# Three taps of one convolution on GpSimd, and the first superblock's weights widened in two halves

## The chip, the cores and the metric

The kernel runs on one core of a Trainium2 chip. The time is that of the whole device program in microseconds, the median of three runs. The engines are named as the profile names them: PE (TensorE matmul), PEld (its weight loads), DVE (VectorE), ACT (ScalarE), POOL (GpSimd), SP (SyncE, which issues the transfers).

## The reference

A causal convolution of seven taps over a sequence, with softmax weights by head (8 heads of 24 channels), is followed by an MLP with a squared ReLU:

```
w = softmax(weight)                    # (8 heads, 7 taps)
out = einsum('hk,bskhg->bshg', w, x_unf)   # x: (8, 4096, 192), padded by 6 in front
h = out.reshape(32768, 192) @ w_in     # 192 x 2048
g = s * relu(h)**2 + b
y = g @ w_out                          # 2048 x 192
```

All of it is float32; the weights of the MLP reach the kernel as the 64-bit words of float64 numbers.

## The kernel before, in words

Each operand of a matmul is split into a high and a low part (`hi`, `lo`, in the type fp32r), and three products (hi by hi, lo by hi, hi by lo) stand for one in float32. The 32768 tokens are worked on in 32 superblocks of 1024 tokens, each of two blocks of 512 columns. The 2048 hidden features are eight pairs of 256. For a block `j` and a pair `p`, `first(n, j, p)` makes the hidden values of 256 features with 18 half-height matmuls into one of two buffers `h`; ACT takes ReLU (`relu`) and the square (`square`); ACT or DVE casts to `qh`; DVE subtracts to get `ql` (`lows`); and `second` (in superblock 0 `second_whole`, ten matmuls) multiplies by `w_out` and accumulates over the pairs. A queue holds the second products back by two items (`LAG`).

Superblock 0 is different from the other 31. Its 90 us hold, beside its own products, the widening of all weights: class `Widen` takes the 64-bit words of one pair (768 columns of words: 384 of `w_in`, 384 of `w_out`) and makes hi and lo. Its steps are `magnitudes` (ACT: absolute value of the upper words into a tile `t`), a clamp to the float32 range (DVE, line 308), two bit operations (DVE, lines 312 and 315; these three are `top`), `his` (ACT: `t` cast into the high half of `W` and `WB`), `low` (DVE, lines 328 and 329) and `los` (DVE, lines 335 and 337, once for `W` and once for `WB`). `W` holds `w_in` and the first 128 output columns of `w_out`, `WB` the last 64. `first(0, j, p)` needs the `w_in` part of pair `p`, `second_whole(0, j, p)` the `w_out` part, `WB` first.

`head` is the start: tap weights by softmax, the convolution of the B channels (64 channels of both blocks, `accB`) on PE as seven float32 products with diagonal matrices, that of block 0's A channels (`acc0`) on DVE as seven operations, and that of block 1's A channels (`acc1`) on PE again, seven products. `split_A` and `split_tensor` make hi and lo of them; `swap` exchanges the two halves of the partitions by transfers (`wA`, `wB`). `pair(p)` then does pairs 2 to 7. `CONV` says how many steps of superblock 1's convolution (17 in all, on DVE) are done in which pair, and `TWICE` names the pairs that have no second products of their own behind them, so that two pairs of `first` follow each other on PE.

DVE, ACT and PE run what is written for superblock 0 in just the order in which it is written (`in_order`); POOL's instructions are placed by the scheduler. An engine executes its own list in order, so an instruction that waits holds all behind it. `raw` holds two tiles `t` and one `c`; `wordp` three tiles of words; `ps_h` two buffers `h`.

Of the kernel before, what the change touches and what calls it, by code (L numbers as in the profile page):

```python
# [9 lines left out]
F32 = mybir.dt.float32  # L10
# [7 lines left out]
P = 128  # L18
# [5 lines left out]
CONV = (0, 1, 1, 1, 1, 1, 4, 8)  # L24
# [13 lines left out]
def conv_attention_then_squared_relu_mlp(  # L38
# [244 lines left out]

    class Widen:
# [15 lines left out]
        def magnitudes(self):  # L300
            self.t = raw.tile([P, CT], I32, name="t")[:, self.lo : self.hi]

            top = words[self.p][:, self.lo : self.hi, 1]
            nc.scalar.activation(self.t.bitcast(F32), top.bitcast(F32), AF.Abs)

        def top(self):
            t, top = self.t, words[self.p][:, self.lo : self.hi, 1]
            nc.vector.tensor_scalar(
                t.bitcast(F32), t.bitcast(F32), TOP_MIN, TOP_MAX, op0=ALU.max, op1=ALU.min
            )  # L310

# [12 lines left out]
        def low(self):  # L324
            low = words[self.p][:, self.lo : self.hi, 0]
            c = raw.tile([P, CT], I32, name="c", bufs=1)[:, self.lo : self.hi]
# [6 lines left out]
        def los(self):  # L333
            for hi, lo, t in self.parts(self.t.bitcast(F32)):
                nc.vector.tensor_tensor(lo, t, hi.bitcast(F32), op=ALU.subtract)
            for _, lo, f in self.parts(self.f):
                nc.vector.tensor_tensor(lo, lo.bitcast(F32), f, op=ALU.add)

        def rest(self):
            self.low()  # L340
            self.los()
# [4 lines left out]
    def fetch(p, a=0, z=None):  # L346
# [19 lines left out]
    nc.vector.reduce_max(tmax, tap, axis=AX.X)  # L366
    nc.vector.tensor_tensor(
        tap, tap, tmax.unsqueeze(2).to_broadcast([P, 2, K]), op=ALU.subtract
    )
    nc.scalar.activation(tap, tap, AF.Exp)  # L370
    nc.vector.reduce_sum(tsum, tap, axis=AX.X)
# [9 lines left out]
    def head():  # L381
# [9 lines left out]
        w0, w0out, w1 = Widen(0, 0, CI), Widen(0, CI, CT), wide[1]  # L391

        def diagonal(w):
            d = act.tile([P, 2, BLK], F32, name="q").rearrange("p a (k f) -> p (a k) f", f=P)
            for k in range(K):
                nc.scalar.activation(d[:, k, :], ident, AF.Identity, scale=w[:, k : k + 1])
            return d

        top, bottom = slice(0, DB), slice(DB, P)
        diagB = diagonal(tapB)  # L400
# [3 lines left out]
        acc0 = xs.tile([P, BLK], F32, name="accA")  # L404
        for _ in one.conv(acc0, one.xA, tapA, BLK):
            pass
        nc.scalar.mul(minus, ident, -1.0)
        diagA = diagonal(tapA)
        w0.magnitudes()
        split = one.split_A(0, acc0)  # L410
        next(split)
        w0.top()
        w0.his()
# [3 lines left out]
        lo = one.split_tensor(accB, hiB, lambda: one.conv_tensor(acc1, diagA, one.xA[:, BLK:], range(0, 2)))  # L417
# [431 lines left out]
```

## Time and profile before

| | |
|---|---|
| time, median of three runs | 2234.87 us (2234.49 to 2235.01) |
| the profiled execution, first to last instruction | 2232.9 us |
| superblock 0, from the first instruction to the first product of superblock 1 | 90.2 us |
| one later superblock of 1024 tokens on PE (two blocks of 34.45 us) | 68.9 us |
| PE busy over the whole span | 2226.4 us |
| DVE, ACT, POOL busy over the whole span | 1753.5, 1286.4, 317.8 us |

The profile was taken on one execution, so its span may differ by some tenths of a microsecond from the runs' median; what lies around the span (start and end of the program) is about 2 us. A row of the timeline gives the start, the duration, the engine, the line of the kernel, the operation with output and inputs, and in brackets the idle time ahead of it with what ended it. Durations of instructions that follow each other on one engine overlap by some hundredths of a microsecond, so that the distance between two starts is what an instruction costs in a full list.

### The profile page before, as it was taken

The numbers are of one execution on the slowest core, as the hardware profiler recorded it, in microseconds if no ns is written. First come the engines' busy times: TensorE is split into PE (matmuls) and PEld (weight loads), VectorE is DVE, ScalarE is ACT, GpSimd is POOL, SyncE is SP. The second block draws the span as 40 slices with busy tenths as digits, with TensorE's granted clock in tenths as the row PEclk, the third lists the DMA queues.
The fourth block names the chain that finished last, engine by engine and source line by source line (L and its number), as shares of the span: only waits on it lengthen the run. The fifth ranks groups of instructions, "written<-read, shape, count | busy, mean of one in ns | idle before, by whom it ended". The sixth has DMA issues, their size and how long they took to land.

```text
span 2232.9 us, 45081 instructions
## 1 busy us (share of the span) xinstructions
PE 2226.4 (100%) x19330; PEld 1829.1 (82%) x19330; DVE 1753.5 (79%) x1995; ACT 1286.4 (58%) x1410; POOL 317.8 (14%) x205
## 2 busy tenths in 40 slices
PE   9999999999999999999999999999999999999999
PEld 6788888888888888888888888888888888888887
DVE  8898778777787787777877878778777787787764
ACT  8755555655555555555555555555655555556554
POOL 0022101111011011110110111111101111011110
PEclk9999999999999999999999999999999999999999
DMA  5113112121121111211111111112121121111110
GB/s 180 34 43 87 40 46 62 48 58 44 44 58 53 53 44 45 56 53 53 43 51 50 53 53 53 48 43 62 51 55 44 44 58 53 53 44 42 46 39 17
DMA packets 46168, 117.51 MB, mean 53 GB/s; under 512 B 7760, under 2 KB 8016, under 8 KB 45968
## 3 DMA queue, kind: packets, MB, share of 16 engines
q1 hardware_dynamic: 45824, 114.50, 18.6%
q8 instruction: 151, 2.47, 0.5%
q14 instruction: 49, 0.40, 0.1%
q10 hardware_dynamic: 144, 0.13, 0.0%
HBM read 31.64 MB, written 25.17 MB: 25 GB/s over the span
## 4 chain that ended last, share of the span: by engine, by line
PE 98%; DVE 1%; ACT 1%; DMA 0%; issue 0%; SPq 0%; DVEq 0%
PE acc L614 50%; PE h L531 46%; DVE accA L163 0%; PE acc L576 0%; ACT q L552 0%; DVE ql L559 0%; PE acc L577 0%; PE acc L583 0%; PE acc L582 0%; PE acc L581 0%; ACT qh L554 0%; ACT q L545 0%; DMA xA<-in_xA 0%; DVE t L315 0%; ACT oC L589 0%
## 5 line engine op out<-in xcount | busy, mean ns | idle before, releaser
L545 ACT ACTIVATE q<-h 128x1024 f32<-128x1024 f32 x512 | 525.5, 1026 | 902.8 <-PE h L531 900.4
L559 DVE TENSOR_TENSOR ql<-q,qh 128x1024 fp32r<-128x1024 f32 x512 | 656.7, 1283 | 56.3 <-ACT qh L554 2.6
L554 DVE CAST qh<-q 128x1024 fp32r<-128x1024 f32 x497 | 370.1, 745 | 395.7 <-ACT q L552 393.3
L614 PE MATMUL acc<-qh,W 64*128 64x512 f32 x3960 | 609.9, 386 | 0.0
L552 ACT ACTIVATE q<-q 128x1024 f32<-128x1024 f32 x512 | 543.6, 1062 | 15.9
L614 PEld LDWEIGHTS acc<-qh,W 64*128 64x128 f32 x3960 | 370.9, 184 | 77.9
L531 PE MATMUL h<-sA,W 64*128 64x512 f32 x3072 | 432.4, 387 | 0.0
L531 PE MATMUL h<-wA,W 64*128 64x512 f32 x3072 | 431.6, 386 | 0.0
L531 PE MATMUL h<-tB,W 64*128 64x512 f32 x1536 | 429.9, 386 | 0.0
L531 PE MATMUL h<-wB,W 64*128 64x512 f32 x1536 | 429.9, 386 | 0.0
L614 PE MATMUL acc<-ql,WB 64*128 64x512 f32 x1980 | 385.7, 386 | 0.4 <-DVE ql L559 0.4
L614 PE MATMUL acc<-qh,WB 64*128 64x512 f32 x1980 | 385.6, 386 | 0.0
L614 PE MATMUL acc<-ql,W 64*128 64x512 f32 x1980 | 385.5, 386 | 0.0
L638 POOL TENSOR_TENSOR oB<-oB,oB 128x512 f32<-128x512 f32 x61 | 115.2, 1889 | 1672.7 <-ACT oB L637 1672.7
L163 DVE SCALAR_TENSOR_TENSOR accA<-xA,tap,accA 128x512 f32<-128x512 f32 x378 | 341.5, 903 | 6.8
L531 PEld LDWEIGHTS h<-sA,W 64*128 64x128 f32 x3072 | 287.3, 184 | 62.9 <-issue 1.1
L531 PEld LDWEIGHTS h<-wA,W 64*128 64x128 f32 x3072 | 287.8, 184 | 60.4
L531 PEld LDWEIGHTS h<-tB,W 64*128 64x128 f32 x1536 | 282.6, 184 | 40.5 <-issue 0.2
L531 PEld LDWEIGHTS h<-wB,W 64*128 64x128 f32 x1536 | 282.5, 184 | 20.1
L614 PEld LDWEIGHTS acc<-ql,WB 64*128 64x128 f32 x1980 | 185.5, 184 | 40.1 <-DVE ql L559 1.3
L614 PEld LDWEIGHTS acc<-ql,W 64*128 64x128 f32 x1980 | 185.5, 184 | 39.0
L614 PEld LDWEIGHTS acc<-qh,WB 64*128 64x128 f32 x1980 | 185.5, 184 | 38.8
(115 smaller groups left out, 1035.4 us busy)
## 6 DMA issues: line engine op xcount, KB each, us to landing
wA<-sA SPq DMA_DIRECT2D x126, 256.0 KB, 3.6
outT<-oA SPq DMA_DIRECT2D x63, 256.0 KB, 2.0
wB<-tB SPq DMA_DIRECT2D x60, 256.0 KB, 3.4
xA<-in_xA SPq DMA_DIRECT2D x24, 515.0 KB, 3.6
xB<-in_xB SPq DMA_DIRECT2D x32, 259.0 KB, 2.6
oC<-oB SPq DMA_DIRECT2D x61, 128.0 KB, 2.2
outT<-oC SPq DMA_DIRECT2D x60, 128.0 KB, 2.3
words<-in_w SPq DMA_DIRECT2D x7, 768.0 KB, 6.2
```

The lines of the kernel that those rows point to most:

```text
L163: nc.vector.scalar_tensor_tensor(acc, src, w[:, k : k + 1], acc, op0=ALU.mult, op1=ALU.add)
L531: nc.tensor.matmul(h[:, i, :], w_in(w, p, chunk[0], rows), chunk[part], start=start, stop=stop)
L545: nc.scalar.activation(q, h, AF.Relu)
L552: nc.scalar.activation(q, q, AF.Square)
L554: cast(qh, q)
L559: nc.vector.tensor_tensor(ql, q, qh.bitcast(F32), op=ALU.subtract)
L614: nc.tensor.matmul(accs[to + 2 * i], w(f, r), q[r, f % 2, :], start=start and f == 0, stop=stop and f == ends[i],)
L638: nc.gpsimd.tensor_tensor(o[1], o[1], o[3], op=ALU.add)
```

## The change

In `head`, three of the seven taps of block 1's A channels (taps 4 to 6) are multiplied and summed by POOL into a tile `rest`; PE does four products with diagonal matrices and a fifth with the identity that adds `rest`. The order around it is new: the low part of block 0, the first high halves and the first of the four products are written in another order, and the high and low halves of pair 1's `w_in` come within `second_block`. The softmax takes the maximum as a bias and the sum from the activation's accumulator.

`Widen` is split: each pair is widened as `w_in` (384 columns) and `w_out` (384 columns) apart, with `top`, `his`, `low` and `los` for each. The clamp becomes a method of its own, `bound`, and is done by POOL for all but the first two `w_in` halves. The last addition of a `w_out` half's `los` (two instructions) is done by POOL too. In `pair(p)` the `w_in` half of the next pair is widened ahead of the `w_out` half of pair `p` itself; before, whole pairs were widened ahead. `CONV` gives pairs 1 and 2 none and the last two one more each.

```diff
-CONV = (0, 1, 1, 1, 1, 1, 4, 8)
+CONV = (0, 0, 0, 1, 1, 1, 5, 9)
+ON_PE = 4
...
+        def bound(self, engine=None):
+            t = raws[self.p][:, self.lo : self.hi].bitcast(F32)
+            (engine or nc.vector).tensor_scalar(
+                t, t, TOP_MIN, TOP_MAX, op0=ALU.max, op1=ALU.min
+            )
...
-        def los(self):
+        def los(self, engine=None):
             for hi, lo, t in self.parts(self.t.bitcast(F32)):
                 nc.vector.tensor_tensor(lo, t, hi.bitcast(F32), op=ALU.subtract)
             for _, lo, f in self.parts(self.f):
-                nc.vector.tensor_tensor(lo, lo.bitcast(F32), f, op=ALU.add)
+                (engine or nc.vector).tensor_tensor(lo, lo.bitcast(F32), f, op=ALU.add)
...
+        for k in range(ON_PE, K):
+            src = x1[:, k : k + BLK]
+            if k == ON_PE:
+                nc.gpsimd.tensor_scalar(rest, src, tapA[:, k : k + 1], None, op0=ALU.mult)
+            else:
+                part = outs.tile([P, BLK], F32, name="oA")
+                nc.gpsimd.tensor_scalar(part, src, tapA[:, k : k + 1], None, op0=ALU.mult)
+                nc.gpsimd.tensor_tensor(rest, rest, part, op=ALU.add)
...
-        one.conv_tensor(acc1, diagA, one.xA[:, BLK:], range(2, K))
+        lo = one.split_tensor(accB, hiB, lambda: on_tensor(range(0, 1)))
+        w0.his()
+        on_tensor(range(1, ON_PE))
+        nc.tensor.matmul(acc1, ident, rest, start=False, stop=True)
...
     def pair(p):
         ha, hb = first(0, 0, p), first(0, 1, p)
+        out = w_out_of[p]
+        out.bound(nc.gpsimd)
+        if p in TWICE:
+            qa, qb = relu(ha), relu(hb)
+            keep(p, 0, *square(qa, nc.scalar.copy))
+            out.top()
+            out.his()
+            out.low()
+            out.los(nc.gpsimd)
+            convolve(CONV[p] // 4)
+            keep(p, 1, *square(qb, nc.scalar.copy))
+            ready(p + 2)
+            convolve(CONV[p] - CONV[p] // 4)
+            return
+        last_pair = p == NPAIR - 1
+        if last_pair:
+            convolve(CONV[p] // 2)
+        else:
+            w_in_of[p + 1].top()
+            w_in_of[p + 1].low()
         qa = relu(ha)
+        if not last_pair:
+            w_in_of[p + 1].his()
+            w_in_of[p + 1].los()
+        two = p + 1 in TWICE
         qa = square(qa, nc.scalar.copy)
+        if not two:
+            keep(p, 0, *qa)
+        out.top()
+        qb = relu(hb)
+        out.low()
+        if two:
+            out.his()
+            out.los(nc.gpsimd)
+            ready(p + 2)
+            keep(p, 0, *qa)
+            qb = square(qb, nc.scalar.copy)
+            after = w_in_of[p + 2]
+            after.top()
+            after.low()
+            after.his()
+            after.los()
+        else:
+            nc.scalar.activation(qb, qb, AF.Square)
+            out.his()
+            out.los(nc.gpsimd)
...
+            ready(p + 2)
```

(`keep` appends an item with its `ql` to the queue; `ready(p)` is `magnitudes` of the whole pair `p` on ACT and `bound` of its `w_in` half on POOL.)

How this moves the instructions is seen at three places. The rows are those of the built programs; a number such as x2 counts equal neighbours, and line numbers differ between the two because the change adds lines.

On PE at the start of the program (`q` is a diagonal matrix, or the identity where the input is `accA`; `sA,W` are the first hidden products). Before:

```order
L257 MATMUL acc_139<-xB,q 128x512 x7
L257 MATMUL acc_140<-xA,q 128x512 x2
L230 MATMUL acc_139<-hiB,minus 128x512
L257 MATMUL acc_140<-xA,q 128x512 x5
L531 MATMUL h<-sA,W 128x512 x6
```

With the change:

```order
L259 MATMUL acc_139<-xB,q 128x512 x7
L438 MATMUL acc_140<-xA,q 128x512
L232 MATMUL acc_139<-hiB,minus 128x512
L438 MATMUL acc_140<-xA,q 128x512 x3
L445 MATMUL acc_140<-accA,q 128x512
L569 MATMUL h<-sA,W 128x512 x6
```

Seven products into `acc_140` have become five, and the last waits for POOL.

On ACT where pair 3 ends and pair 4 begins (`t<-words` are the magnitudes of pair 5, `W<-t` its high half, `q<-h` the ReLU of pair 4's two blocks, the other rows square and cast). Before:

```order
L304 ACTIVATE t<-words 128x768
L545 ACTIVATE q<-h 128x1024
L552 ACTIVATE q<-q 128x1024
L554 CAST qh<-q 128x1024
L322 CAST W<-t 128x640
L322 CAST WB<-t 128x2x64
L545 ACTIVATE q<-h 128x1024
L304 ACTIVATE t<-words 128x768
L545 ACTIVATE q<-h 128x1024
```

(the ReLU in the second row is still pair 3's, and the last magnitudes are those of pair 6). With the change:

```order
L309 ACTIVATE t<-words 128x768
L590 ACTIVATE q<-q 128x1024
L592 CAST qh<-q 128x1024
L332 CAST W<-t 128x384
L583 ACTIVATE q<-h 128x1024 x2
```

In both, pair 4's ReLUs stand behind the high half of pair 5. Before, three rows lay between its magnitudes and that high half, with DVE's three operations beside them; now two rows, with POOL's clamp and DVE's two bit operations beside them.

On DVE in pairs 6 and 7, the last of superblock 0 (`ql` is the low part of a hidden block, `accA` and `accB` are steps of superblock 1's convolution). Before:

```order
L559 TENSOR_TENSOR ql<-q,qh 128x1024
L163 SCALAR_TENSOR_TENSOR accA<-xA,tap,accA 128x512
L559 TENSOR_TENSOR ql<-q,qh 128x1024
L163 SCALAR_TENSOR_TENSOR accA<-xA,tap,accA 128x512
L180 TENSOR_TENSOR sA<-accA,sA 128x512
L161 TENSOR_SCALAR accB<-xB,tap 128x512
L163 SCALAR_TENSOR_TENSOR accB<-xB,tap,accB 128x512 x3
L559 TENSOR_TENSOR ql<-q,qh 128x1024
L163 SCALAR_TENSOR_TENSOR accB<-xB,tap,accB 128x512 x2
L559 TENSOR_TENSOR ql<-q,qh 128x1024
```

With the change, pair 6 and then, after the first steps into `accB`, pair 7:

```order
L597 TENSOR_TENSOR ql<-q,qh 128x1024
L322 TENSOR_SCALAR t<-t 128x384
L325 SCALAR_TENSOR_TENSOR t<-words,t 128x384
L338 TENSOR_SCALAR c<-t 128x384
L339 SCALAR_TENSOR_TENSOR c<-words,c 128x384
L345 TENSOR_TENSOR W<-t,W 128x256
L345 TENSOR_TENSOR WB<-t,WB 128x2x64
L165 SCALAR_TENSOR_TENSOR accA<-xA,tap,accA 128x512
L597 TENSOR_TENSOR ql<-q,qh 128x1024
L165 SCALAR_TENSOR_TENSOR accA<-xA,tap,accA 128x512 x3
L182 TENSOR_TENSOR sA<-accA,sA 128x512
```

```order
L597 TENSOR_TENSOR ql<-q,qh 128x1024
L322 TENSOR_SCALAR t<-t 128x384
L325 SCALAR_TENSOR_TENSOR t<-words,t 128x384
L338 TENSOR_SCALAR c<-t 128x384
L339 SCALAR_TENSOR_TENSOR c<-words,c 128x384
L345 TENSOR_TENSOR W<-t,W 128x256
L345 TENSOR_TENSOR WB<-t,WB 128x2x64
L165 SCALAR_TENSOR_TENSOR accB<-xB,tap,accB 128x512 x2
L597 TENSOR_TENSOR ql<-q,qh 128x1024
```

The `w_out` halves of pairs 6 and 7, six instructions each, now stand among the last low parts and the convolution; before, DVE had done them within pairs 4 and 5.

157 lines of the change are left out of this document (81 added, 76 removed).

## The prediction

> **What bounds the kernel now.** The page first: PE is busy in every slice. Then the windows by stage, which show where other engines are as full.
>
> ```profile
> PE 2226.4 (100%) x19330; PEld 1829.1 (82%) x19330; DVE 1753.5 (79%) x1995; ACT 1286.4 (58%) x1410; POOL 317.8 (14%) x205
> 17.30:31.70 14.40, 14.00 (x94) 10.54 (x93) 14.12 (x27) 13.59 (x19) 0.00 (x0) 1.00 0.82 280
> 67.90:90.10 22.20, 22.20 (x133) 17.83 (x132) 19.18 (x26) 16.41 (x19) 0.00 (x0) 1.00 0.13 35
> 165.00:2165.00 2000.00, 2000.00 (x17652) 1652.92 (x17650) 1572.91 (x1744) 1133.05 (x1223) 295.60 (x186) 1.00 0.19 51
> ```
>
> From 165 us on PE never idles, and the change touches nothing there. All it can move lies ahead of 90.2 us, in superblock 0, where DVE is 98% busy (14.12 of 14.40) at first and PE still idles 0.4. The chain of waits says how little room is there: it starts on DVE, not on PE, and leaves PE again at 72.34 for ACT and DVE until past 100 us.
>
> ```profile
> 5.06 0.50 DVE accA L161
> 14.06 0.48 DVE t L308
> 18.72 0.50 PE acc L230
> 67.97 4.35 PE h L531 x36
> 72.34 1.03 ACT q L545
> 79.40 0.62 ACT sA L178
> 86.27 1.22 DVE ql L559
> 90.12 0.69 ACT oA L587
> ```
>
> So PE is full, but without slack to DVE and ACT at the start (the low halves of the first weights) and in the tail of superblock 0. Those are the places the change rewrites.
>
> **The head, PE's side.** Five float32 products last from 12.96 to the start of the hidden products at 17.34, 0.88 us each; two fewer save 1.75. Between its first six products and the next, PE also waits for ACT's copy of `acc1` (18.72), about 0.8 us, which the new order can remove. At best 2.6.
>
> ```profile
> 12.96 4.46 PE L257 MATMUL acc<-xA,q 128*128 128x512 f32 x10
> 17.34 0.98 PE L531 MATMUL h<-sA,W 64*128 64x512 f32 x6
> 18.72 0.50 PE L230 MATMUL acc<-sA,minus 128*128 128x512 f32 x1 [0.40 <-ACT sA L227]
> 20.64 0.84 PE L531 MATMUL h<-sA,W 64*128 64x512 f32 x6
> ```
>
> **What POOL costs DVE.** POOL has not run beside DVE in superblock 0 so far. Later rows show both together:
>
> ```profile
> 1716.63 1.88 POOL L638 TENSOR_TENSOR oB<-oB,oB 128x512 f32<-128x512 f32 x1 [28.56 <-ACT oB L637]
> 1718.48 1.48 POOL L642 TENSOR_TENSOR oA<-oA,oA 128x512 f32<-128x512 f32 x1
> 1717.28 1.52 DVE L191 CAST hiB<-accB 128x512 fp32r<-128x512 f32 x1
> 135.07 0.41 DVE L191 CAST hiB<-accB 128x512 fp32r<-128x512 f32 x1
> 168.98 1.72 POOL L518 TENSOR_SCALAR oB<-oB,bias 64x512 f32<-64x512 f32 x1
> 162.00 3.07 DVE L163 SCALAR_TENSOR_TENSOR accA<-xA,tap,accA 128x512 f32<-128x512 f32 x3
> 81.18 2.33 DVE L163 SCALAR_TENSOR_TENSOR accB<-xB,tap,accB 128x512 f32<-128x512 f32 x3
> 167.49 1.78 DVE L180 TENSOR_TENSOR sA<-accA,sA 128x512 fp32r<-128x512 f32 x1
> ```
>
> An addition on POOL holds a DVE operation back by 1.1 us (1.52 against 0.41). A product with a scalar costs less: over four of them DVE loses 0.74 (3.07 against 2.33), 1.1 (1.78 for a subtraction of 0.69) and some tenths more on two others, about 0.6 each. By length I put a clamp of 384 columns at 0.45 of DVE's time and 1.25 of POOL's (1.67 between the starts at 512 columns; the lower end is 0.35, DVE's own), the two additions of 256 and 128 columns at 0.8 of DVE's and 1.1 of POOL's (from 1.48).
>
> [...]
>
> **The head, DVE's side.** DVE's list runs unbroken from 5.06, through block 0's convolution, to the low half of pair 0's `w_in` at 14.06. POOL can start when the second half of `xA` has landed:
>
> ```profile
> 1.65 3.28 DMA xA<-in_xA
> 2.60 0.43 SPq L153 DMA_DIRECT2D xA<-in_xA  x1
> xA<-in_xA SPq DMA_DIRECT2D x2, 256.0 KB, 3.8
> ```
>
> Two such transfers have a median of 3.8, and the first took 3.3, so the second took 4.3 from 2.60: 7.0 with the wake-up. Three products of 1.7 and two additions of 1.5 to 1.9 end near 16, so PE's fifth product ends near 17, not at 15.3: most of the 1.75 is spent there. DVE loses 3 x 0.6 + 2 x 1.1 = 4.0, and up to 2 x 0.45 for the clamps behind: low half at 18 to 19. Pair 1's `w_in` half follows:
>
> ```profile
> 10.19 0.35 DVE L308 TENSOR_SCALAR t<-t 128x384 f32<-128x384 f32 x1
> 10.97 0.56 DVE L315 SCALAR_TENSOR_TENSOR t<-words,t 128x384 int32<-128x384 int32 x1
> 12.05 0.35 DVE L328 TENSOR_SCALAR c<-t 128x384 int32<-128x384 int32 x1
> 13.50 0.56 DVE L337 TENSOR_TENSOR W<-W,c 128x384 fp32r<-128x384 f32 x1
> ```
>
> 1.3 (10.19 to the end at 11.5) and 2.0 (12.05 to 14.06) are 3.3: ready at 21.3 to 22.3. PE needs it at the fifth product of its second block, 0.45 behind 20.64 so far. That is +0.2 to +1.2; up to 1.0 more comes from ACT, whose cast of that half waits for DVE ahead of the copies that feed the second block's transfers. Ends: -2.6 (POOL blocks nothing) and +2.2. I take **+0.5**, since some blocks will fall on DVE's own waits.
>
> **Two pairs in a row on PE.** Behind pair 4, and again behind pair 6 (`TWICE`), the next pair's first product needs the buffer that ReLU frees, and ReLU stands behind the next pair's high half on ACT.
>
> ```profile
> 51.46 0.73 ACT L322 CAST W<-t 128x640 fp32r<-128x640 f32 x1 [0.40 <-DVE t L315]
> 52.37 1.03 ACT L545 ACTIVATE q<-h 128x1024 f32<-128x1024 f32 x1
> 54.21 1.03 PE L531 MATMUL h<-sA,W 64*128 64x512 f32 x6
> 54.74 0.18 PEld L531 LDWEIGHTS h<-sA,W 64*128 64x128 f32 x2 [0.34 <-DVE W L337]
> ```
>
> Before, that ReLU ended 0.8 ahead of PE's start at 54.21. Now DVE first widens the `w_out` half of pair 3, 0.8 + 0.9 + 0.5 = 2.2 us (by the rows above, 256 and 128 columns at 0.3 and 0.2); only then is a tile `t` free for pair 5's magnitudes. POOL does 1.1 of additions, then the clamp, 1.25; DVE 0.9; ACT's cast 0.45 and ReLU 1.05. That is 7.0 from the end of pair 4's `w_in` half. If that half is just in time for PE's pair 4, PE comes back after two blocks, 4.3 us (67.97 to 72.3), and waits 2.7; each microsecond that DVE is ahead takes one off. Ends 0 and 3.3; I take **+2.5** at each place, 5.0 together. This also bounds the gain: what PE saves in the head it gives back here, since DVE is not earlier by it.
>
> **The tail.** Pairs 6 and 7 get the `w_out` halves that DVE had done in pairs 4 and 5.
>
> ```profile
> 75.44 1.23 DVE L559 TENSOR_TENSOR ql<-q,qh 128x1024 fp32r<-128x1024 f32 x1 [1.06 <-ACT qh L554]
> 79.93 1.02 ACT L545 ACTIVATE q<-h 128x1024 f32<-128x1024 f32 x1
> 83.42 1.22 DVE L559 TENSOR_TENSOR ql<-q,qh 128x1024 fp32r<-128x1024 f32 x1
> 85.55 0.39 PE L576 MATMUL acc<-qh,WB 128*128 128x512 f32 x1
> 90.17 0.97 PE L531 MATMUL h<-sA,W 64*128 64x512 f32 x6
> ```
>
> Before: pair 7's first low part ends at 84.6, PE takes it at 85.55. Now, on the same chain: pair 6's `w_out` half puts its two bit operations (0.9) and ACT's cast (0.55) ahead of pair 6's second square, which with its low part comes 1.5 to 2.5 later; two more convolution steps stand ahead of `sA` (2 x 0.75), and ReLU of pair 7 behind it: low part 3.5 later. Behind it come pair 7's own `w_out` half, 2.2, and POOL's additions, 1.1, without which PE's product with `WB` cannot start. 3.5 + 3.3 - 0.95 of slack = 5.9, less what fell on idle time: **+5.5** (4.5 to 6.1). Last, ACT's final copy into `wB` now stands behind the output scaling that waits for the last product: **+0.8** (0 to 1.6) at the start of superblock 1. Nothing later gives it back: PE has no idle time there.
>
> **Sum.** 0.5 + 5.0 + 5.5 + 0.8 = 11.8 us, on a span of 2232.9: 2244.7. The runs' median is 2.0 above that span: **2246.7**. Moved for nothing: the softmax (DVE waits for `xA` until 5.06 anyway), the split of 768 into two 384 (some 0.5 a pair more) against the clamp and two additions less (1.1 a pair), which the blocks of 1.7 a pair outweigh.
>
> **The rivals.** *POOL is quick and blocks little.* Its clamps and additions are then near DVE's own times, the head keeps 2.6 and the place behind pair 4 costs nothing; behind pair 6 1.6 remains, and the tail with 4.5 to 5.5: +3.5 to +6, about 2239. For it: clamps with constants are not in the trace. Against: 1.72 for 512 columns. *DVE is blocked for POOL's whole record*: the head +4 to 5 more and the pairs a little, 16 to 21 in all, 2254. Against it, 1.52 against 0.41. [...] *PE stays the bound, on the other side*: the queue of two items hides the lateness of the tail, and two products and the wait are gone: -1.7 to -2.6, about 2232.6. It decides if pair 7's `w_out` half is ready within 1 us of its low part; DVE's list puts 2.2 and POOL 1.1 there. That the change does not do what it says is part of the first sum: POOL's `rest` comes after PE's four products.
>
> **How the numbers follow.** Forecast (+7 to +16) 0.57; POOL quick 0.18; whole-record block 0.10; PE stays the bound 0.15. What this kernel's measurement can tell from no change is about 0.2%, 4.5 us. Within it lie nearly all of the last and a third of the second: 0.19. Faster by more needs 4.5, more than the 2.6 there is: 0.02. Slower: 0.79. The range leaves out part of the gain below and half the whole-record case above: 2238 to 2254.
>
> **What would show it.** In the head: DVE's convolution of block 0 stretched beyond its 4.69, the fifth product near 16 and the first hidden product near 17, with PE waiting for a low half of `W`. Behind pairs 4 and 6: PE idle 2 to 3 us, released by ReLU. In the tail: PE idle 5 to 6 us at the first product with `WB` of pair 7, released by POOL. Wrong if PE's hidden products of superblock 1 start at or before 92, or if DVE keeps its durations beside POOL.

## The result and the profile after

The changed kernel takes 2257.5 us (median of four runs, 2256.5 to 2259.1) against 2234.8 (2234.5 to 2235.0): the ratio is 1.0102, with a 95% interval of 1.009 to 1.0114. It is slower by 22.7 us, where 11.8 had been forecast. The profiled execution is the run of 2259.1, 1.6 above the median; its span is 2257.4.

The loss lies where it was looked for, ahead of superblock 1: its first hidden product starts at 113.46 in place of 90.17. TensorE's waits up to 120 us, in the table of waits of the changed kernel (total, times, longest):

```profile
PE acc L614 <- POOL WB L347: 7.0, 2, 5.2
PE h L569 <- ACT q L583: 5.3, 2, 2.7
PE acc L445 <- POOL accA L421: 2.3, 1, 2.3
```

The same waits in the timeline of its PE (start, duration, operation, idle time ahead with what ended it):

```profile
17.33 1.18 PE L445 MATMUL acc<-accA,q 128*128 128x512 f32 x2 [2.31 <-POOL accA L421]
50.98 0.50 PE L614 MATMUL acc<-qh,WB 128*128 128x512 f32 x1 [1.85 <-POOL WB L347]
64.46 1.08 PE L569 MATMUL h<-sA,W 64*128 64x512 f32 x6 [2.67 <-ACT q L583]
86.83 1.65 PE L569 MATMUL h<-sA,W 64*128 64x512 f32 x6 [2.63 <-ACT q L583]
107.16 0.80 PE L614 MATMUL acc<-qh,WB 128*128 128x512 f32 x1 [5.19 <-POOL WB L347]
113.46 0.97 PE L569 MATMUL h<-sA,W 64*128 64x512 f32 x6
116.07 0.50 PE L569 MATMUL h<-wB,W 64*128 64x512 f32 x2 [0.95 <-ACT wB L216]
```

The gaps behind pairs 4 and 6 and the one in the tail have the forecast sizes. They are less than half of the loss. The ReLUs of superblock 0 on ACT show where the rest went. Before (pair 1's second block, pair 3's second block, the first block of pair 4 and of pair 7, superblock 1):

```profile
31.73 1.01 ACT L545 ACTIVATE q<-h 128x1024 f32<-128x1024 f32 x1
47.89 1.00 ACT L545 ACTIVATE q<-h 128x1024 f32<-128x1024 f32 x1
52.37 1.03 ACT L545 ACTIVATE q<-h 128x1024 f32<-128x1024 f32 x1
79.93 1.02 ACT L545 ACTIVATE q<-h 128x1024 f32<-128x1024 f32 x1
93.03 1.02 ACT L545 ACTIVATE q<-h 128x1024 f32<-128x1024 f32 x1
```

The same five in the changed kernel (pair 6's first ReLU, between, went from 70.30 to 85.76):

```profile
34.12 1.02 ACT L583 ACTIVATE q<-h 128x1024 f32<-128x1024 f32 x1
56.21 1.02 ACT L583 ACTIVATE q<-h 128x1024 f32<-128x1024 f32 x1
63.39 1.93 ACT L583 ACTIVATE q<-h 128x1024 f32<-128x1024 f32 x2
98.73 1.02 ACT L583 ACTIVATE q<-h 128x1024 f32<-128x1024 f32 x1
117.76 1.03 ACT L583 ACTIVATE q<-h 128x1024 f32<-128x1024 f32 x1 [1.74 <-PE h L569]
```

The lag grows from 2.4 (34.12 less 31.73) to 8.3 over pairs 2 and 3, where the forecast had nothing, to 11.0 at pair 4, 18.8 at pair 7 and 24.7 at superblock 1. What DVE does meanwhile is in the windows (DVE is the third busy time). Before, from 15 to 75 us and up to the first product of superblock 1:

```profile
15.00:75.00 60.00, 59.60 (x385) 45.09 (x385) 57.16 (x89) 54.16 (x68) 0.15 (x1) 1.00 0.35 122
0.00:90.17 90.17, 88.62 (x484) 63.51 (x484) 80.60 (x127) 75.78 (x106) 1.03 (x9) 1.00 0.36 120
```

Changed:

```profile
15.00:75.00 60.00, 53.08 (x300) 39.13 (x300) 45.52 (x76) 42.27 (x56) 29.27 (x24) 0.89 0.38 124
0.00:113.46 113.46, 97.46 (x480) 68.89 (x481) 87.17 (x143) 75.95 (x113) 46.02 (x44) 0.91 0.30 96
```

Two readings. DVE does not get less to do: it is busy for 87.2 us up to that product, 6.6 more than before, though clamps and additions have left it. And it idles 26.3 us (113.46 less 87.17) in place of 9.6: before, it was busy for 57.2 of the 60 us, nearly as full as PE (59.6); now for 45.5. The table of DVE's waits names the largest part:

```profile
DVE t L322 <- POOL t L315: 9.2, 6, 1.8
```

So DVE waits for POOL's clamp in six of the pairs. One more column had not been looked for: the granted clock (the number behind POOL's, 1.00 in every row of before). In the changed kernel it falls to half at five of the six gaps of PE (not at the one of 0.95 us):

```profile
19.00:25.00 6.00, 6.00 (x27) 4.00 (x25) 3.57 (x8) 3.59 (x7) 1.40 (x1) 0.50 0.70 154
52.00:56.00 4.00, 4.00 (x12) 3.12 (x11) 3.43 (x7) 2.22 (x3) 1.84 (x2) 0.57 0.01 5
66.00:70.00 4.00, 4.00 (x25) 3.13 (x24) 3.04 (x7) 1.81 (x4) 0.00 (x0) 0.57 0.00 0
86.50:90.00 3.50, 3.17 (x16) 2.52 (x18) 2.88 (x5) 3.18 (x4) 0.00 (x0) 0.51 0.00 0
107.00:111.00 4.00, 3.84 (x10) 3.08 (x11) 3.20 (x4) 0.00 (x0) 0.10 (x1) 0.57 0.02 4
```

The mean clock of 0.995 over the span of the profiled execution (0.996 and 0.997 in the other three) is 11 us' worth of full speed (0.005 x 2257), about what the forecast lacked. That made half speed the first suspect.

### The profile page after: what moved, and what is told of

It reads as the page before. It is cut to its first block, busy times and chain, and to the rows that moved or that the text cites. A ratio compares the mean times of both kernels' runs of the same rounds, so it can differ in the third digit from the quotient of the medians.

```text
span 2257.4 us, 45150 instructions
## 1 busy us (share of the span) xinstructions
PE 2235.8 (99%) x19326; PEld 1838.8 (81%) x19326; DVE 1760.6 (78%) x2012; ACT 1285.8 (57%) x1417; POOL 363.6 (16%) x240
## 4 chain that ended last, share of the span: by engine, by line
PE 95%; DVE 2%; POOL 1%; ACT 1%; DMA 0%; issue 0%; SPq 0%; DVEq 0%; POOLq 0%; ACTq 0%
PE acc L652 50%; PE h L569 45%; POOL t L315 0%; DVE ql L597 0%; DVE t L325 0%; POOL WB L347 0%; ACT q L590 0%; DVE t L322 0%; DMA xA<-in_xA 0%; ACT q L583 0%; POOL W L347 0%; ACT qh L592 0%; DVE c L339 0%; POOL oA L420 0%; DVE W L345 0%
## 5 line engine op out<-in xcount | busy, mean ns | idle before, releaser
L597 DVE TENSOR_TENSOR ql<-q,qh 128x1024 fp32r<-128x1024 f32 x512 | 660.7, 1291 | 57.2 <-ACT qh L592 3.7
```

What stands on the lines that cost most here:

```text
L597: nc.vector.tensor_tensor(ql, q, qh.bitcast(F32), op=ALU.subtract)
```

## The experiments

Times are medians, beside runs of the kernel before on the same chip (2234.6 to 2234.8 each time). Runs of one kernel lie within 2.7 us of each other, most within 1.

### Is it the clock?

Matmuls that multiply zeros into the accumulators fill PE's gaps (8 + 7 + 10 + 10 + 21; the sum in the expectation should read 56):

```diff
+        zeros_into(acc1, 8)
         nc.tensor.matmul(acc1, ident, rest, start=False, stop=True)
...
+        zeros_into(a2, ZEROS.get((j, p), 0))    # {(0, 1): 7, (0, 7): 21}
...
+        if p - 1 in TWICE:
+            zeros_into(acc[0, 0][0], 10)
```

> The changed kernel (2257.5 us), with 46 matmuls of 128 x 512 added that multiply zeros into the accumulators, put where its trace has TensorE idle while it waits: 8 before the fifth product of block 1 (the gap of 2.31 us), 7 before the wait of 1.85 us near 51 us, 10 before the first products of pairs 5 and 7 (2.67 and 2.63 us), 21 in the gap of 5.2 us near 102 us. At 0.227 us each they fill 1.8, 1.6, 2.3, 2.3 and 4.8 us and leave at most 0.5 us idle. Theory A (the time at half clock adds to the idle time): the granted clock stays at 1.00 in all five places, some 20 us at 0.50 go, and about half of them, 8 to 10 us, come off: 2247.5 to 2249.5. Theory B (the loop of the widening over ScalarE, GpSimd and VectorE sets the pace and the slow products are hidden in it): the clock is 1.00, too, but the gaps behind it grow by what the products gain; only what is lost behind the last gap (about 1.7 us) comes off: 2255 to 2257. Rival C (the clock is not what the idle time drags down): the rows of the clock stay as they were, and the time at 2257.5 or above.

Measured: 2254.4 us (ratio 1.0089, 1.0073 to 1.0104), mean clock 0.999, with half speed left only behind a gap of 1.78 us behind pair 4. That is 3.1 us less, not 8 to 10, and 0.6 us below theory B's range. Theory B holds for most of it: the slow products are hidden in waits for something else. By this run the clock's own price is about 3 us of 22.7.

### The parts of the change taken apart

The clamps and last additions go back to DVE in their places (`bound()`, `los()`); then the three taps go back to PE; then both, which leaves the new order with `w_in` and `w_out` apart and nothing on POOL:

```diff
-        out.bound(nc.gpsimd)
+        out.bound()
...
-ON_PE = 4
+ON_PE = 7
...
-        nc.tensor.matmul(acc1, ident, rest, start=False, stop=True)
```

> The changed kernel with the clamps and the last additions of the widening back on VectorE, in the same places of the order; GpSimd keeps the three taps. VectorE gets 14 clamps of 384 columns at 0.36 us and 7 times 0.70 us of additions more, about 10 us, and loses the 9.2 us in which it waits for GpSimd's clamp and some 7 us by which its instructions are longer beside GpSimd. Theory A (the way through GpSimd is what costs): the gaps of 1.85, 2.67, 2.63 and 5.2 us shrink below 1 us each, only the head's gap and its half clock stay, and the time is 2240 to 2245. Rival (w_out in a half of its own and late is what costs, wherever it runs): the last gap stays at 4 us or more and the time at 2252 or above.

> The changed kernel with all seven products of block 1's first convolution on TensorE again (no taps and no sum on GpSimd); the widening as changed. TensorE's gap of 2.31 us before the fifth product goes, and the half clock from 18.4 to 25 us with it; two products of 0.88 us come back. If idle time and half clock add up: 2.3 + 3.3 - 1.8 = 3.8 us less, 2253.7. If the loop of the widening sets the pace from 25 us on: within 1 us of the changed kernel, 2256.5 to 2258. If GpSimd's taps delay VectorE's convolution of block 0 and all that follows it: 0.3 us for its seven instructions, about 2257.

> The changed kernel without GpSimd: seven products on TensorE, clamps and additions on VectorE. What is left of the change is w_in and w_out widened apart, with w_out late (and the softmax of the taps). Theory A (GpSimd's part costs 15 us or more): 2236 to 2241. Rival (the order and the halves cost by themselves: per pair two instructions of 384 columns for one of 768, 0.16 us more for each of five, 0.8 us a pair and 6 us in all, and the last w_out halves wait at the end): 2245 or above, with a gap of 3 us or more near the end of the first superblock.

Measured: clamps and additions on DVE 2249.5 (1.0067, 1.0052 to 1.0082); taps on PE 2257.3 (1.0101, 1.0084 to 1.0118); both 2249.05 (1.0065, 1.005 to 1.008). In the first run the time lies between the two theories, with the last gap at 5.47 us as the rival has it; in the third the rival won, and the second stayed within 1 us of the changed kernel. The order by itself, without POOL, costs 14.4 us (in it are the halves and the new softmax, which was not run alone), and POOL another 8.4, of which 8.0 are its part in the widening. Within this order the taps are worth nothing either way (0.2, with runs that overlap). In the run with the order alone, the windows and the waits of DVE are:

```profile
0.00:102.55 102.55, 91.01 (x486) 64.75 (x486) 86.59 (x173) 76.47 (x116) 1.03 (x9) 0.97 0.34 106
```

```profile
DVE ql L587 <- ACT qh L582: 3.3, 6, 0.9
DVE W L345 <- ACT W L332: 2.0, 1, 2.0
DVE t L315 <- ACT t L309: 1.7, 4, 0.4
```

The first product of superblock 1 comes 12.4 us later than before (102.55 less 90.17). By the same row DVE is busy 6.0 us more (86.59 less 80.60) and idle 6.4 more (15.96 against 9.57), part of it in new waits for ACT's cast in the head (2.0) and for the magnitudes (1.7); the wait for casts to `qh` was 2.6 before. By the ReLUs this kernel is 1.8 us late at pair 3's second block, 5.5 at pair 6 and 13.8 at superblock 1: more than half of what the order costs arises behind pair 6.

### Two halves for one whole

Nothing but the halves, in the old order without POOL, in two forms: the two halves of an instruction side by side, or the whole chain of `w_in` and then the whole chain of `w_out`, in which each instruction needs the one before it:

```diff
+            for r in self.cuts():            # both halves of one instruction, then the next
+                nc.vector.tensor_scalar(t[:, r], t[:, r], 3, 0x3FFFFFFF, ...)
```

```diff
+            for w in map(self.sub, self.both()):   # clamp, shift, merge of w_in, then of w_out
+                nc.vector.tensor_scalar(t, t, 3, 0x3FFFFFFF, ...)
```

> The kernel before, in its old order, with nothing on GpSimd; each VectorE instruction of a whole pair's widening is issued as two (columns of w_in, columns of w_out) right behind one another. By the rows of before and of the run without GpSimd: clamp, shift and mask 0.36 x 2 for 0.555, the two scalar-tensor-tensors 0.558 x 2 for 0.959, subtraction and addition 0.557 + 0.416 for 0.819: 0.165 x 3 + 0.157 x 2 + 0.154 x 2 = 1.12 us a pair and 7.8 us for seven pairs. Theory A (VectorE's sum of work sets the end of the first superblock once the order is changed; it is the halves that make it longer): VectorE is busy 80.6 us up to the first product of superblock 1 now and 88 us then, the time is 2238 to 2242, and the halves explain a third to a half of the 14.4 us that the run without GpSimd lost. Rival (VectorE has slack in the old order and only the new order, with w_out late, costs): 2234.5 to 2236.

> The kernel before, in its old order, nothing on GpSimd. VectorE's work on a whole pair is issued as two chains, as in the changed kernel: first clamp, shift and merge of the w_in columns and then of the w_out columns, so that each instruction needs the one just before it. The run with the two halves of one instruction side by side made VectorE only 1.2 us busier, since they overlap. Theory A (a chain of dependent halves costs the whole 0.16 us for each extra instruction, and VectorE's sum of work decides): VectorE is busy for 87 to 88.6 us up to the first product of superblock 1, as in the run without GpSimd (88.6), and the time is 2238 to 2242. Rival (the old order has slack for that, and it is the order alone, w_out late and block 1's convolution later, that costs the 14.4 us): VectorE is as busy, TensorE hardly waits, 2234.5 to 2236.5.

Measured: side by side 2234.8 us, no difference (1.0, 0.999 to 1.0009); as dependent chains 2238.25 (1.0016, 1.0006 to 1.0025). The windows up to the first product of superblock 1, side by side:

```profile
0.00:90.23 90.23, 88.82 (x484) 63.67 (x484) 81.87 (x176) 75.69 (x106) 1.04 (x9) 1.00 0.36 120
```

and as chains:

```profile
0.00:95.31 95.31, 91.10 (x484) 64.03 (x484) 86.04 (x176) 75.86 (x106) 1.03 (x9) 1.00 0.35 114
```

As many instructions (x176) in both; side by side they overlap (two clamps of 384 columns last 0.62 us together, in the chains 0.354 each) and make DVE 1.3 us busier, in chains 5.4. So the extra work that theory A expected of the first run never arose, and only the second run tests it. There the 5.4 us appear as 5.1 us of delay in the profiled execution, which was the slowest (2239.4), and as 3.5 by the medians: **in superblock 0, DVE has some two microseconds of slack, not ten.** Most of its 9.6 us of idle time lies outside the 60 us in which it was busy for 57.2.

### POOL at work beside DVE, with nobody waiting for it

```diff
+            if self.p:
+                whole = W[:, self.p, 0, 0:GAP].bitcast(F32)
+                for _ in range(2):
+                    nc.gpsimd.tensor_scalar(spare, whole, TOP_MIN, TOP_MAX, ...)
+                for _ in range(2):
+                    nc.gpsimd.tensor_tensor(spare, whole, spare, op=ALU.add)
```

> The kernel before, in its old order, with four GpSimd instructions added behind the widening of each of pairs 1 to 7 (two clamps and two additions of 296 columns, some 5 us a pair as in the changed kernel). They read that pair's finished weights and write a spare buffer that nobody reads, so no engine waits for them and no work is taken off VectorE. Theory A (a good part of what GpSimd costs is that VectorE's instructions last longer beside it): VectorE is 4 to 8 us busier up to the first product of superblock 1 (80.6 us before; in the changed kernel the 16 subtractions for the low parts took 1.36 us in place of 1.22, the shift 0.50 in place of 0.36), and the time is 2236 to 2240. Rival (only the waits for GpSimd's results cost): VectorE at 80 to 82 us busy, 2234.5 to 2235.5.

Measured: 2243.5 us (1.0039, 1.0025 to 1.0054), 8.9 us slower, more than either theory had. POOL is nearly as busy as in the changed kernel (42.2 us against 46.0), and DVE by 11.4 us more than before:

```profile
0.00:98.99 98.99, 90.52 (x484) 63.22 (x484) 91.97 (x127) 75.36 (x105) 42.24 (x37) 1.00 0.34 109
```

The groups of its DVE instructions (form, count, total, mean ns):

```profile
L567 DVE TENSOR_TENSOR ql<-q,qh 128x1024 fp32r<-128x1024 f32 x16 | 20.9, 1309 | 0.2 <-ACT qh L562 0.2
L337 DVE TENSOR_TENSOR WB<-WB,c 128x128 fp32r<-128x128 f32 x8 | 5.9, 733 | 0.0
L308 DVE TENSOR_SCALAR t<-t 128x768 f32<-128x768 f32 x7 | 5.1, 730 | 0.0
```

and before:

```profile
L559 DVE TENSOR_TENSOR ql<-q,qh 128x1024 fp32r<-128x1024 f32 x16 | 19.5, 1220 | 2.7 <-ACT qh L554 2.6
L337 DVE TENSOR_TENSOR WB<-WB,c 128x128 fp32r<-128x128 f32 x8 | 2.3, 283 | 0.0
L308 DVE TENSOR_SCALAR t<-t 128x768 f32<-128x768 f32 x7 | 3.9, 553 | 0.0
```

The small addition takes 0.73 us in place of 0.28, the clamp 0.73 in place of 0.55. Over 28 instructions of POOL, 14 clamps and 14 additions of 296 columns whose results nobody reads, that is 0.41 us of DVE's time for each (11.4 / 28), and less in all than POOL's records last: 41 us (42.24 less the 1.03 of before). In the changed kernel the clamps and additions that left DVE were worth about as much as this takes back: with them on DVE it is busy 89.5 us up to the first product of superblock 1, with them on POOL 87.2.

### The taps alone, in the old order

Three taps on POOL in the kernel before; the same with the fifth product behind the first six hidden products; the same and ACT's copy of block 1 ahead of its casts of pair 1:

```diff
+        for k in range(ON_PE, K):            # as in the changed kernel, into rest
...
+            nc.tensor.matmul(acc1, ident, rest, start=False, stop=True)   # now in second_block
             lo1 = one.split_tensor(acc1, sA[:, 0, :])
             one.swap(wA[:, 0, :], sA[:, 0, :])
+            w1.his()                          # and w1.low(), w1.los() ...: behind the copy
```

> The kernel before with three taps of block 1 on GpSimd and five products on TensorE, as in the changed kernel; the softmax and the widening of all weights as before. If the sum of GpSimd is late as in the changed kernel (17.3 us), TensorE waits about 2 us before the fifth product, two products of 0.88 us less make up for most of that, and the clock then falls to half for 3 to 7 us, which costs 1.7 to 3.3 us where TensorE is the bound as it is in before: 2236.5 to 2238.5. If GpSimd slows VectorE in the head more than that: above 2239. If neither gap nor clock matters, as putting the taps back onto TensorE hardly moved the changed kernel: 2234 to 2235.5.

> The same as the run with the taps alone, but the fifth product (identity times GpSimd's sum) is issued behind the first six hidden products, which need neither the sum nor block 1. They are about 1 us of work and fill the wait. If the wait of about 2 us and the half clock behind it are what the taps cost: a gap below 1 us, the clock at 1.00, and 1 to 2.5 us less than the taps alone, 2233.5 to 2236, which is the two products saved at best. If VectorE beside GpSimd is what is late (w_in of pair 0): the first hidden products are late themselves and the time stays with the taps alone.

> The kernel before with three taps on GpSimd, the fifth product behind the first six hidden products, and in addition ScalarE's copy of block 1 ahead of its casts of pair 1's weights (the changed kernel has it so), since the trace of the run before this one has TensorE wait 3.4 us for that copy, which stands behind a cast that waits for VectorE. If that wait is what the taps cost in the old order: TensorE's wait falls below 1.5 us, the clock stays at 1.00, 2234 to 2236. If VectorE beside GpSimd is what costs (its last addition for pair 0 took 1.62 us in place of 0.56, its clamp for pair 1 1.63 in place of 0.55): the wait moves to the products that need pair 1's weights, 2237 to 2240.

Measured: 2239.6 (1.0023, 1.0014 to 1.0032), 2239.9 (same interval) and 2237.7 us (1.0015, 1.0006 to 1.0025). Moving the fifth product gave nothing, since PE's longest wait was for ACT's copy of block 1 (3.4 us), behind a cast that waits for DVE. With the copy ahead, 2 us come back, and PE waits 2.16 us for pair 1's weights instead. Behind these waits (4.06, 3.41 and 2.16 us in the three runs) the granted clock was at half for 3.4, 6.8 and 3.4 us, so part of each loss is half speed; it was not taken apart. What is late first is DVE beside POOL, in the second of these runs:

```profile
14.34 1.62 DVE L339 TENSOR_TENSOR W<-W,c 128x384 fp32r<-128x384 f32 x1
15.88 1.63 DVE L310 TENSOR_SCALAR t<-t 128x768 f32<-128x768 f32 x1
```

The same two before:

```profile
13.50 0.56 DVE L337 TENSOR_TENSOR W<-W,c 128x384 fp32r<-128x384 f32 x1
13.97 0.55 DVE L308 TENSOR_SCALAR t<-t 128x768 f32<-128x768 f32 x1
```

Each is 1.1 us longer (1.62 for 0.56, 1.63 for 0.55), and POOL's two additions last from 14.27 to 17.09 beside them. In the old order, where DVE is full, that counts; in the new one, where it idles later anyway, taking the taps back gained nothing. The ReLUs of the new order show where the difference is lost: with the taps on PE, and with the taps on POOL and PE's gaps filled, the first ReLU of pair 2 is 0.2 and 0.7 us later than before, and the second 3.2 in both, as DVE waits for POOL's clamp in between; from there on the two stay together up to pair 7 (16.4).

### The shared buffer and the late `w_out`

In the changed kernel one tile `t` holds the magnitudes of both halves of a pair. ACT cannot take those of pair p+2 before `w_out` of pair p is done, so subtraction, magnitudes, clamp, shift and merge follow one another in every pair. One experiment gives each half rings of its own; one widens `w_out` of pairs 6 and 7 a pair sooner; one does both; two more do the first and both without POOL:

```diff
-                raws[self.p] = raw.tile([P, CT], I32, name="t")
+            raws[self.p, self.lo] = raw.tile([P, CI], I32, name="t" if self.lo else "ti")
...
         qa = relu(ha)
+        ready(p + 2)                          # was behind out.los(nc.gpsimd)
```

```diff
             after.los()
+            if p == 5:
+                out = w_out_of[6]             # bound, top, his, low, los here; pair 7's in pair 6
```

> The changed kernel with a buffer ring of its own for the magnitudes of w_in and one for those of w_out (384 columns each, two buffers each, in the place of two of 768). ScalarE takes the magnitudes of w_in of pair p+2, and GpSimd clamps them, right behind the first ReLU of pair p, where the changed kernel has them behind the whole widening of w_out of pair p, since they share its buffer. ScalarE pays 0.56 x 2 for 0.91 a pair. Theory A (the loop sets the pace: subtraction for w_out, then magnitudes 0.9, clamp 1.5, shift and merge 1.0, all one behind another in every pair): VectorE's waits of 9.2 us for GpSimd's clamp fall below 3 us, the gaps behind pairs 4 and 6 get shorter, and the time is 2248 to 2252. Rival (the sum of VectorE's work with its stretches beside GpSimd is what sets the end): VectorE's waits go but are replaced by later ones, 2255 or above.

> The changed kernel with the w_out halves of pairs 6 and 7 widened one pair sooner (pair 6's at the end of pair 5, pair 7's in pair 6 in the place of pair 6's own). Nothing else is moved and no work is added. If the late w_out of pair 7 is what TensorE waits for at the end: the gap of 5.2 us at 102 us falls below 1.5 us, and with it the half clock of 107 to 110 us (1.7 us): 2251 to 2253. If the sum of VectorE's work up to the first product of superblock 1 (87.2 us) sets the end, TensorE waits for the convolution of superblock 1 instead, or earlier for w_in of pair 7: at most 2 us less, 2255.5 to 2258.

> The changed kernel, GpSimd as changed, with both: buffer rings of their own, and w_out of pairs 6 and 7 one pair sooner. The rings alone gave 4.3 us, the earlier w_out alone 2.4, with the gaps behind pairs 4 and 6 grown to 4.3 and 4.8 us. If the two hinder one another because the earlier w_out has to pass the shared buffer: together more than their sum, 2246 to 2250. If VectorE's work with its stretches sets the end: about the better of the two, 2251.5 to 2254.

> The new order without GpSimd (2249.05 us) and with the buffer rings of their own for the magnitudes of w_in and w_out, so that those of w_in of pair p+2 are taken behind the first ReLU of pair p. If the shared buffer costs by the order alone, too: VectorE's waits for ScalarE's magnitudes and casts (1.7 and 2.0 us there) go, 2245.5 to 2247.5. If it costs only because GpSimd's clamp of 1.5 us stands in the loop (4.3 us there): 2248 to 2250.

> The same as the run with rings of their own and without GpSimd, and w_out of pairs 6 and 7 widened one pair sooner in addition. Theory A (what the order costs beyond the 3.5 us of dependent halves is the shared buffer and the late w_out of the last pair, which TensorE awaits for 5.5 us): both waits gone, 2238.5 to 2243. Rival (VectorE's work sets the end, wherever w_out is put): within 2 us of the same without the earlier w_out, and the wait turns up before pair 7 or superblock 1.

Measured with POOL: own rings 2253.3 (1.0082, 1.0067 to 1.0097), earlier `w_out` 2255.1 (1.0092, 1.0075 to 1.0109), both 2250.4 (1.007, 1.0055 to 1.0085). Without POOL: own rings 2248.1 (1.006, 1.0045 to 1.0075), both 2247.2 (1.0056, 1.0041 to 1.0071). With rings of their own DVE's waits for the clamp fall from 9.2 to 3.2 us (theory A had asked for less than 3, and for a time of at most 2252):

```profile
DVE ti L325 <- POOL ti L318: 3.2, 2, 1.8
```

and 4.3 us come off: the loop is real. Without POOL the same edit gives 1.0, so the loop cost mainly because POOL's clamp, at 1.5 us for 384 columns, stood in it. The earlier `w_out` mostly moves the wait: with POOL it takes PE's wait of 5.2 us away and only 2.4 us of the time, as the waits behind pairs 4 and 6 grow to 4.3 and 4.8. Both edits with POOL took 7.1 us, about the sum of the two, between what the two theories had said. With both edits and no POOL, the 5.4 us for which PE awaited the last `WB` are gone, but PE then waits longer for ReLU behind pair 6 (3.6 us, where it was 0.2; behind pair 4 it is 1.7 against 1.9):

```profile
PE h L563 <- ACT q L577: 5.3, 2, 3.6
```

0.9 us is gained, which is the rival's case: the work on DVE has to be done, wherever `w_out` is put. If the parts add up, 3.5 of the order's 14.4 us are the dependent halves as measured alone, and about 2 the rings and the last `w_out`. The rest, some 9 us, was not taken apart by runs: that it goes with the new waits between ACT and DVE, and with work that DVE catches up on in the tail, fits the rows but is not shown. No version here beats the kernel before.

## Why the prediction was wrong

The direction was right, and the size was wrong by the factor of 1.9 (22.7 for 11.8); the range of 2238 to 2254 did not hold it.

- **The step that failed** is the last sentence of the sum, "Moved for nothing: ... the split of 768 into two 384 (some 0.5 a pair more) against the clamp and two additions less (1.1 a pair), which the blocks of 1.7 a pair outweigh". By the ReLUs of the two profiled executions, the 24.7 us by which superblock 1 is late divide into 2.4 for the head up to pair 1's second block (forecast 0.5), 7.9 in pairs 2, 3 and 5 (forecast nothing), 5.2 at the places behind pairs 4 and 6 (forecast 5.0) and 9.3 in the tail (forecast 6.3). So the nothing became the largest miss. It arises between the two ReLUs of a pair: ACT's cast of the high half of the next pair's `w_in` stands between them now, and waits 3.1, 3.0 and 2.2 us there in pairs 2, 3 and 5 for DVE, which itself waits for POOL's clamp, as in pair 2:

```profile
42.72 0.51 ACT L332 CAST W<-t 128x384 fp32r<-128x384 f32 x1 [3.08 <-DVE t L325]
```

  In the run with the order alone that wait in pair 2 is 2.2 us, and 5.0 of the 7.9 are there too. The balance of work had the right sign, but was too large: 1.1 us a pair against DVE are 7.7 for seven pairs, and DVE became 4.2 us busier with the taps on PE (84.75 up to the first product of superblock 1 in that run), 6.6 with all of POOL's work. What was wrong was to price it at nothing. The windows of before had shown DVE at 98% from 17 to 32 us, and over 15 to 75 us it is at 95%, so there was little cover. The runs with dependent halves and with idle work on POOL show it: 5.4 us more on DVE cost 3.5 by the medians, 11.4 cost 8.9. Work is the smaller part, though: of the 23.3 us by which the first product of superblock 1 comes later (113.46 less 90.17), 6.6 are more work on DVE and 16.7 more idle time of DVE, of which 9.2 are its waits for the clamp.
- **The wait for the clamp**, in the same place, was seen as a chain, "only then is a tile `t` free for pair 5's magnitudes", but priced behind pairs 4 and 6 alone, where PE waits at once. DVE waits for it in six pairs, 9.2 us in all. The rings of their own brought back 4.3.
- **The two places behind pairs 4 and 6**, +2.5 each: 2.67 and 2.63. Right, in size and releaser.
- **The tail**, +5.5 and +0.8: the gaps are 5.19, released by POOL's `WB`, and 0.95, released by ACT's `wB`. Right as gaps. But the second ReLU of pair 7 to the first of superblock 1 grew by 5.92 us, and pair 6 to pair 7 by another 3.34: 9.3 together, where the forecast had 6.3 in all. The run with the order alone has 8.3 there, so POOL is not the main cause.
- **The head**, +0.5: +2.9 at the first ReLU in the profiled run (23.71 less 20.85), outside the ends. POOL started at 8.73 instead of 7.0, since its part of `xA` took 5.9 us to land rather than 4.3; `rest` came at 17.27, not 16; half speed then lasted to 25 us. The last of these decides: five runs that have the three taps on POOL, but whose clock stayed at 1.00 there (gaps filled, clamps on DVE, own rings, earlier `w_out`, both), are late by only 0.1 to 0.8 at that ReLU, and in one of them (clamps on DVE) `rest` came as late, at 17.25. Without half speed the +0.5 was right, although `rest` was late.
- **The prices of POOL.** Blocking: 1.7 us of DVE a pair forecast, 1.6 measured with idle work on POOL (11.4 / 7). POOL's own speed was too good in the forecast: a clamp of 384 columns is 1.5 us rather than 1.25, and the two additions 2.0 rather than 1.1:

```profile
L315 POOL TENSOR_SCALAR t<-t 128x384 f32<-128x384 f32 x14 | 21.0, 1514 | 2.1 <-ACT t L309 2.1
L347 POOL TENSOR_TENSOR WB<-WB,c 128x128 fp32r<-128x128 f32 x8 | 9.0, 1125 | 0.0
L347 POOL TENSOR_TENSOR W<-W,c 128x256 fp32r<-128x256 f32 x8 | 7.0, 875 | 47.3 <-DVE W L345 47.3
```

- **The rivals.** "DVE is blocked for POOL's whole record" gave 2254, the nearest number, for a reason that the rows refute (11.4 us of DVE for 41 us of POOL's records with idle work on POOL). So the number is near by luck. "POOL is quick and blocks little" fell with the clamp's 1.5 us. "PE stays the bound" fell with the first gap.
- **Half speed** stood in no term. It is seen at five gaps, and 3.1 us came off in the run that took most of it away.

## What to carry to other kernels

Before a step is priced at nothing, read the busy share of the engine that is to absorb it over just that stretch: an engine at 95% there passed on 3.5 of 5.4 us and 8.9 of 11.4, although it idled for 9.6 us in the stage, most of it at the ends. Work moved from DVE to POOL has to be worth more than the 0.4 us of DVE that each POOL instruction took here, and whoever reads POOL's result gets a step of 1.5 us into its chain, so that what frees the buffer for it must not wait at the end of the same pair. Where a long instruction is cut in two, issue the halves side by side: here they overlapped so, and 49 extra instructions cost DVE 1.3 us; in two dependent chains the same 49 cost it 5.4, 0.11 each.

## What the hardware showed that was not expected

A deliberate series of gaps shows when the granted clock fell. The kernel before got extra ReLUs on ACT at one step in each of superblocks 4 to 29:

```diff
+            if (j, p) == (0, 3) and 4 <= n < 30:
+                for _ in range(6 + n // 2):
+                    nc.scalar.activation(q[:, 0, :], h[:, 0, :], AF.Relu)
```

> The kernel before with extra ReLUs of 128 x 512 on ScalarE at one step in each of superblocks 4 to 29 (8 in superblock 4 to 20 in superblock 29), which repeat the step's own ReLU and change nothing in the result. ScalarE has some 2 us of slack in a step of 4.3 us and TensorE is two steps ahead, so TensorE should be idle for nothing at 8 and up to some 8 us at 20. If the granted clock falls to half behind each gap beyond a length: no drop in the first superblocks, one in each of the later ones, with the limit between 1.6 us (a gap without a drop in the run with the taps back on TensorE) and 2.8 us. If the place of the gap decides and not its length alone, as the gaps of 2.8 and 2.3 us without a drop in the run without GpSimd suggest: drops and none mixed over gaps of 2 to 3.5 us, and a drop behind every gap beyond that. Each drop of 3.4 us at half clock costs 1.7 us beside its gap.

It took 2311.9 us in a single run. PE's gaps came in pairs of nearly equal length, as here, in the timeline of its PE:

```profile
1294.11 0.50 PE L531 MATMUL h<-sA,W 64*128 64x512 f32 x2 [1.89 <-ACT q L790]
1366.08 0.50 PE L531 MATMUL h<-sA,W 64*128 64x512 f32 x2 [1.89 <-ACT q L790]
```

Around the first the clock stays at 1.00; behind the second it is at half for most of the 4 us from 1367:

```profile
1292.00:1301.00 9.00, 6.53 (x54) 4.91 (x54) 5.61 (x8) 7.60 (x10) 0.00 (x0) 1.00 0.00 0
1367.00:1371.00 4.00, 4.00 (x24) 2.92 (x22) 3.65 (x5) 3.21 (x5) 0.00 (x0) 0.57 0.00 0
```

No gap up to 1.26 us brought the clock down; one of two of 1.89 did, one of two of 2.5, and all eight of 3.15 to 5.04. Half speed then lasted 3.4 us, or twice that in three of the ten cases, and it began as early as before the gap's end and as late as 1.5 us after it. So the length of the gap alone did not decide here.

The trace shows what goes with it. The ten drops begin at 1367.58, 1439.26, 1586.02 us and so on up to 2111.68, and each distance between two of them is, within 0.02 us, a whole multiple (21 to 43 times) of 3.413 us; the 744.10 us from the first to the last are 218 such stretches. In the changed kernel, too, the five drops (18.27, 52.40, 66.05, 86.53, 107.01) lie 10, 4, 6 and 6 such stretches apart. So in these two profiles every drop lies on a grid of 3.413 us, and what tells a gap with a drop from one without is how long PE idles within one stretch of it. The first gap of 1.89 us falls into two stretches, with 1.62 us in the second of them; the other falls into one stretch whole, and the drop comes at that stretch's end, 1367.58:

```profile
1292.49:1295.90 3.41, 1.79 (x16) 1.49 (x18) 0.69 (x1) 3.32 (x5) 0.00 (x0) 1.00 0.00 0
1364.17:1367.58 3.41, 1.52 (x16) 1.24 (x16) 0.43 (x1) 3.32 (x5) 0.00 (x0) 1.00 0.00 0
```

Counted so in these two profiles, with the grid laid through the first drop (up to 130 us in the changed kernel, from 300 us on in the series of gaps), a stretch at full clock with 1.82 us or more of idle PE was followed by half speed each time (15 stretches), one with 1.64 or less never, and the two of 1.76 and 1.78 were not, although in the run with PE's gaps filled half speed followed a gap of 1.78. So about half a stretch idle was enough here; the ends of PE's products are modelled, so this limit may be off by a little. It fits the gaps of 2.8 and 2.3 us in the run with the order alone, each cut in two by the grid through that run's drop (1.63 and 1.16, 1.17 and 1.09), which left the clock at 1.00, and the one of 1.85 in the changed kernel, which lay in one stretch and brought it down. In the head, the changed kernel's gap of 2.31 us lay in one stretch, and the run with the clamps on DVE had one of 2.04 with at most 1.11 in one stretch: the first brought the clock down, the second did not.
